# Sparse attention into a token mix: stores and loads of x by 32 rows, a second tile of normalised sums, another order of heads, and the mix's first steps in the attention's written order

## The chip, the cores and the metric

One core of one Trainium2 chip. The metric is device microseconds of one execution; lower is better. A core has TensorE (PE, with its weight loads PEld), VectorE (DVE), ScalarE (ACT), GpSimd (POOL) and SyncE (SP), which here only issues DMAs. All of them run their own queue in order and meet at semaphores.

## The reference

```python
scores = scale * np.matmul(q, k.transpose(0, 1, 3, 2))      # 4 batches, 8 heads, 768 x 64
mask = np.abs(blk_i - blk_j) <= 1                            # blocks of 32: 24 of them
mask |= (blk_i == 0) | (blk_j == 0) | (blk_i == 23) | (blk_j == 23)
# and three sampled key blocks for every query block
attn = softmax(where(mask, scores, -1e9));  x = attn @ v     # x: 4 x 768 x 512, heads side by side
theta = x @ w_theta;  zr, zi = x * cos(theta), x * sin(theta)
y = einsum('ts,bsd->btd', w_tok_r, zr) + einsum('ts,bsd->btd', w_tok_i, zi)
u = x + y;  out = u + np.maximum(u @ w_ch, 0.0)
```

## The kernel before

**Attention.** Two batches and eight heads are worked on together (bp = 0, 1). The eight heads are four positions p with two halves e each. A *unit* is one query block i of 32 rows (i = 1 to 22) over at most eight key blocks, or a *wide* unit: the first and last query block, which see all 768 keys, for one batch b and two positions. Per bp there are four wide units, then 22 units that go in pairs (odd i, then even i). The loop over n (from L449) is written out by hand under `manual_schedule()`, and each engine's queue has exactly this order. In an iteration: `load_q` (SP); `gather_k` of unit n+2 (POOL copies kg<-kb, L243); `scale_q` (DVE, L217); `scores` of unit n+1 (PE, S, L282, then the minimum m on DVE, L285); for odd i `values` of the pair before (PE, X, L333); `weights` of unit n+1 (ACT, exponentials P, L294); `turn` of unit n (PE transposes T, L300, and the ACT copy to pT, L302); a share of decoding the mix's weights (`Decoder`, pieces of 512 KB loaded at L59, then DVE and ACT); `finish` of the pair before; `load_pair` (va, SP, L262) and `gather_v` (vb, an indirect DMA of POOL, L265).

`finish` normalises X on DVE into the tile xo (L315 to L319, one buffer, `bufs=1`) and stores it to the DRAM tensor xs by two DMAs, one for each half c of the partitions (L350). Each has 64 rows of 2 KB, and its DRAM side has as its outermost dimension the two query blocks. `finish_wide` does the same for the wide units (L405), with the first and the last block outermost. X has one buffer as well, T one, S two, pT one, vb four, va two.

The layout of xs is `[bp, block, c, 32 rows, b, pp, 128]` with p = 2 pp + c. Keys come by `load_k` (L222) into kb, one buffer for the bp's 3 MB: the loads for bp = 1 stand at the top of the iteration in which the unit after next is the first wide one, behind the stores of the pair before, and wait for POOL's last copy out of the old keys.

**Mix.** `token_mix` is a generator. Its first part, up to the `yield`, loads x for steps 0 and 1 (`load_raw`: tile xr, four DMAs, L560; `load`: tile xa, four DMAs of 128 rows of 512 bytes with four blocks as outermost dimension, L547), transposes xr on DVE (`turn`, L576, then ACT and DVE for the high and low part), loads ACT's Sin table (L534) and does `theta` (PE, h, L586 to L588). A step is 128 tokens and 256 channels; there are 48. The attention calls this part at its end, after it has given back kb's and the scores' memory (L513, L514); there the written order no longer holds, and a planner places the instructions by its own estimates, also between those of the attention's last iterations. The rest of the mix (`mix`, PE, y, L624 to L626; `out`, L647 to L649) follows under the planner, in memory that the attention's other tiles leave.

`Tables` prepares the sampled block numbers at the start, in tiles of its own (DVE on sb_raw, L149 to L167).

Of the kernel before, what the change touches and what calls it, by code (L numbers as in the profile page):

```python
# [24 lines left out]
VB_BUFS = 4  # L25
Q_BUFS = 3
RAW_AHEAD = 6

# [88 lines left out]
class Tables:  # L117


    def __init__(self, nc, cp, sampled):  # L120
        self.raw = cp.tile([P, NB * 6], I32, name="sb_raw")
        nc.sync.dma_start(self.raw, sampled.rearrange("i k -> (i k)").partition_broadcast(P))

    def make(self, nc, cp):
        raw = self.raw
        words = raw.rearrange("p (i k w) -> p i k w", k=3, w=2)
        given = cp.tile([P, 3, NB], F32, name="sb_given")
        nc.vector.tensor_copy(given, words[:, :, :, 0].rearrange("p i k -> p k i"))
        r = cp.tile([P, 3, NB], F32, name="sb_r")
# [3 lines left out]
        iota_i = cp.tile([P, NB], I32, name="iota_i")  # L133
        nc.gpsimd.iota(iota_i, pattern=[[1, NB]], base=0, channel_multiplier=0)
        qi = cp.tile([P, NB], F32, name="qi")
# [6 lines left out]
        first_i = cp.tile([96, NP], I32, name="first_i")  # L142
        for k in range(3):
            nc.gpsimd.iota(first_i[32 * k : 32 * k + 32], pattern=[[768, NP]], base=0, channel_multiplier=1)
        first = cp.tile([96, NP], F32, name="first_row")
        nc.gpsimd.tensor_copy(first, first_i)

        u, t = raw.bitcast(F32).rearrange("p (x k i) -> x p k i", x=2, k=3)
        nc.vector.tensor_tensor(u, r, given, op=ALU.not_equal)  # L149
        nc.vector.tensor_tensor(t, r, qi.unsqueeze(1).to_broadcast([P, 3, NB]), op=ALU.subtract)  # L150
        nc.vector.tensor_tensor(t, t, t, op=ALU.mult)
        nc.vector.scalar_tensor_tensor(u, t, 1.5, u, op0=ALU.is_lt, op1=ALU.max)
        nc.vector.scalar_tensor_tensor(t, r, float(NB - 1), r, op0=ALU.subtract, op1=ALU.mult)
        nc.vector.scalar_tensor_tensor(u, t, 0.0, u, op0=ALU.is_equal, op1=ALU.max)
        for k in range(1, 3):
            for j in range(k):
                nc.vector.tensor_tensor(t[:, j, :], r[:, k, :], r[:, j, :], op=ALU.is_equal)
                nc.vector.tensor_tensor(u[:, k, :], u[:, k, :], t[:, j, :], op=ALU.max)

        for k in range(3):  # L160
            g = slice(32 * k, 32 * k + 32)
            nc.vector.tensor_scalar(t[g, 0, :], u[g, k, :], -1.0, 1.0, op0=ALU.mult, op1=ALU.add)
            for bp in range(NP):
                nc.vector.tensor_scalar(t[g, 1 + bp, :], r[g, k, :], 32.0, first[g, bp : bp + 1], op0=ALU.mult, op1=ALU.add)
        left, base = t[0:96, 0:1, :], t[0:96, 1:3, :]
        nc.vector.scalar_tensor_tensor(base, base, -ZEROS, left.to_broadcast([96, NP, NB]), op0=ALU.add, op1=ALU.mult)
        nc.vector.tensor_scalar(rows[0:96], base, ZEROS, None, op0=ALU.add)  # L167


def attention(tc, qT, qE, kT, vr, sampled, xs, ident, pieces, follow):  # L170
# [8 lines left out]
    nc = tc.nc  # L179
    with ExitStack() as ctx, ExitStack() as early:  # L180
# [3 lines left out]
        ps_s = early.enter_context(tc.tile_pool(name="ps_s", bufs=2, space=PSUM, side="right"))  # L184
        gp = ctx.enter_context(tc.tile_pool(name="gp", bufs=1))
# [33 lines left out]
        def load_k(bp, b, pp):  # L219
            if (b, pp) == (0, 0):  # L220
                kbs[bp] = kp.tile([P, 8, NB, 32], F32, tag="kb", name=f"kb{bp}")
            nc.sync.dma_start(kbs[bp][:, 4 * b + 2 * pp : 4 * b + 2 * pp + 2], kT[bp, b][:, 2 * pp : 2 * pp + 2])  # L222

        def load_edges(bp):
# [47 lines left out]
        def scores(bp, i):  # L272
# [5 lines left out]
            for b in range(2):  # L278
                for p in range(4):
                    for e in range(2):  # L280
                        rows = slice(64 * e, 64 * e + 64)
                        nc.tensor.matmul(sc[32 * p : 32 * p + 32, e, b, :], q[rows, b, p, :], keys[rows, :, :, 4 * b + p, :], start=True, stop=True)  # L282
            m = wp.tile([P, 2, 2], F32, tag="m", name=f"m{bp}_{i}", bufs=3)
# [28 lines left out]
        def normalised(name, x, n):  # L312
# [3 lines left out]
            nc.vector.reciprocal(sm, sm)  # L316
            xo = wp.tile([P, 8, 64], F32, tag="xo", name=f"xo{name}", bufs=1)[:, 0:n]
            by = sm.rearrange("r (b g) -> r b g", g=4).unsqueeze(3).to_broadcast([P, n // 4, 4, 64])
# [8 lines left out]
        def values(bp, i):  # L327
            x = st[bp, i]["X"] = sums_tile(f"{bp}_{i}")
            va = vas[((i - 1) // 2) % VA_BUFS]
            def weigh(b, e, p, c, u0, n, v, start, stop):  # L330
                r0 = 64 * (p % 2) + 32 * u0
                v0 = 65 * (8 * b + 4 * (p // 2) + 2 * e + p % 2)
                nc.tensor.matmul(  # L333
                    x[r0 : r0 + 32 * n, b, 2 * (p // 2) + e, :], pT_pair[:, 4 * c + 2 * e + b, p, u0 : u0 + n, :], v[:, v0 : v0 + 65],
                    start=start, stop=stop,
                )

            for e in range(2):
                for pp in range(2):
                    heads = [(b, e, 2 * pp + c) for b in range(2) for c in range(2)]  # L340
                    for head in heads:
# [5 lines left out]
        def finish(bp, i):  # L347
            xo = normalised(f"{bp}_{i}", st.pop((bp, i))["X"], 8)
            for c in range(2):
                nc.sync.dma_start(xs[bp, i : i + 2, c].rearrange("u q b p f -> u q (b p f)"), xo[64 * c : 64 * c + 64])  # L350

# [8 lines left out]
        def scores_wide(bp, b, pp):  # L360
            qe, kb = qes[bp], kbs[bp]
            scs = [ps_s.tile([P, 2, 2, 256], F32, tag="S", name=f"SW{bp}_{b}{pp}{e}").rearrange("r x y f -> r (x y f)") for e in range(2)]
            for c0, n in ((0, 16), (16, 8)):
                for c in range(2):
                    for e in range(2):
                        rows, p = slice(64 * e, 64 * e + 64), 2 * pp + c
                        nc.tensor.matmul(  # L367
                            scs[e][64 * c : 64 * c + 64, 32 * c0 : 32 * (c0 + n)], qe[rows, b, p, :], kb[rows, 4 * b + p, c0 : c0 + n, :],
                            start=True, stop=True,
# [29 lines left out]
        def finish_wide(bp, b, pp):  # L399
            if b == 0:  # L400
                load_v_wide(bp, 1, pp)
            if pp == 1:
                xo = normalised(f"{bp}_w{b}", xws[bp][:, b : b + 1], 4)
                for c in range(2):
                    nc.sync.dma_start(xs[bp, 0 : NB : NB - 1, c, :, b].rearrange("z q p f -> z q (p f)"), xo[64 * c : 64 * c + 64])  # L405

# [27 lines left out]
        with tc.manual_schedule():  # L434
            load_edges(0)
            load_k(0, 0, 0)
            tab = Tables(nc, cp, sampled)
            turn_edges(0)
# [9 lines left out]
            do(0, weights, weights_wide)  # L448
            for n in range(len(units) + 1):  # L449
                phases = 0  # L450
                if n < len(units):
# [40 lines left out]
                else:  # L492
# [9 lines left out]
                    else:  # L502
                        turn(bp, i)
                        do(n + 1, weights, weights_wide)
                    decoder.go(phases)
                    if last:
                        finish(*last)
# [4 lines left out]
            assert not decoder.left(), decoder.left()  # L512
        early.close()  # L513
        next(follow)  # L514


def token_mix(tc, w, ch_pieces, xs, outT, bias, nb):
# [8 lines left out]
    with ExitStack() as late, ExitStack() as ctx:  # L526
        xp = ctx.enter_context(tc.tile_pool(name="xp", bufs=3, side="right"))
        tz = ctx.enter_context(tc.tile_pool(name="tz", bufs=2, side="right"))
        tps = [ctx.enter_context(tc.tile_pool(name="tp0", bufs=1, side="right"))]
        ps_h = ctx.enter_context(tc.tile_pool(name="ps_h", bufs=3, space=PSUM, side="right"))  # L530
        ps_o = ctx.enter_context(tc.tile_pool(name="ps_o", bufs=1, space=PSUM, side="right"))

        half_pi, up_int, down_int, early = bias
        tc.keep_in_program_order(nc.scalar.activation(early, half_pi, AF.Sin))  # L534
        xa, xr, xT, angles, zs, us, ys = {}, {}, {}, {}, {}, {}, {}
# [5 lines left out]
        def load(k):  # L541

            b, h, j = at(k)
            xa[k] = xp.tile([P, 4, 4, 32], F32, tag="xa", name=f"xa{k}")
            for p in range(4):
                src = xs[b // 2, 4 * j : 4 * j + 4, p % 2, :, b % 2, p // 2]
                nc.sync.dma_start(xa[k][:, p].rearrange("s c u -> s (c u)"), src)  # L547

        def load_raw(k, pool=None):
# [8 lines left out]
            for p in range(4):  # L558
                src = xs[b // 2, 4 * j : 4 * j + 4, p % 2, :, b % 2, p // 2].rearrange("i q c -> q i c")
                nc.sync.dma_start(xr[b, j][32 * p : 32 * p + 32].rearrange("r i c u -> r i (c u)"), src)  # L560
# [95 lines left out]
        for k in range(2):  # L656
            load_raw(k, xp)
            load(k)
        turn(0)
        turn(1)  # L660
        theta(0)
        theta(1)
# [122 lines left out]
```

## Time and profile before

| what | value |
|---|---|
| median of the three runs shown | 686.46 us (680.64, 686.46, 686.54) |
| time of the profiled execution | 681.48 us |
| its span (first to last instruction) | 679.7 us |
| mean granted TensorE clock | 0.924 |
| busy: PE, PEld, DVE, ACT, POOL | 576.1, 501.7, 448.6, 334.9, 140.6 us |
| moved by DMA | 95.57 MB, mean 141 GB/s |

All rows below are of that one execution, in us from the span's start. In the groups a row reads: line, engine, operation, tile written <- tiles read, shapes, count | busy us, mean ns of one | idle us just before them, and what ended that idle time. The chain of waits is followed back from the last instruction: start, duration, what. A timeline row is start, duration, engine, line, operation, with the idle time before it in brackets. A stretch (A:B) gives its length, then busy us and count of each engine, the granted clock, the mean busy share of the DMA engines, and GB/s.

### The profile page before, as it was taken

The page shows a single profiled execution, that of the slowest core. Times are in us where ns is not written, and L with a number is a line of the kernel's source. Part 1 is how long each engine was busy: PE and PEld are TensorE (multiplying, and loading weights), DVE is VectorE, ACT ScalarE, POOL GpSimd, SP SyncE. Part 2 cuts the span into 40 slices and gives each one's busy share as a digit, 9 for nine tenths or more (in the row PEclk, how much of TensorE's full clock was granted, in tenths as well). Part 3 has the DMA queues.
Part 4 walks back from the last instruction along what each step waited for, and adds up shares of the span by engine and source line. Part 5 has one row for each costly group of instructions (what it writes and reads, how often), then busy time and mean ns, then how long its engine had stood idle before and what let it go on. Part 6 is the DMA issues. An engine that isn't in the chain of part 4 may idle for free.

```text
span 679.7 us, 16671 instructions
## 1 busy us (share of the span) xinstructions
PE 576.1 (85%) x6592; PEld 501.7 (74%) x6592; DVE 448.6 (66%) x1063; ACT 334.9 (49%) x708; POOL 140.6 (21%) x262
## 2 busy tenths in 40 slices
PE   4788767585878777774879999999999999999996
PEld 2466445462655545543769999999999999999996
DVE  3797775463777657655389979666586765846654
ACT  3466546362656455544266575345553455533520
POOL 1457546322247454620000000000000000000000
PEclk9989789786989879995769999999999999999999
DMA  8778668665579656742344323421133211121102
GB/s 300 257 224 237 212 208 261 219 213 191 175 231 274 194 180 201 250 140 78 92 123 120 107 56 83 123 78 59 48 95 108 68 58 47 60 69 62 31 0 94
DMA packets 71110, 95.57 MB, mean 141 GB/s; under 512 B 5240, under 2 KB 52984, under 8 KB 71032
## 3 DMA queue, kind: packets, MB, share of 16 engines
q1 hardware_dynamic: 64696, 71.08, 33.3%
q0 software_dynamic: 6336, 23.43, 10.6%
q8 instruction: 52, 0.85, 0.5%
q14 instruction: 26, 0.21, 0.1%
HBM read 81.90 MB, written 12.58 MB: 139 GB/s over the span
## 4 chain that ended last, share of the span: by engine, by line
PE 48%; DMA 34%; DVE 10%; SPq 3%; ACT 3%; issue 2%; DVEq 0%; ACTq 0%
DMA xs<-xo 26%; PE y L624 9%; PE y L625 9%; PE y L626 9%; PE h L588 3%; PE h L586 3%; PE h L587 3%; PE o L647 3%; PE o L648 3%; PE o L649 3%; PE SW L367 3%; DMA kb<-in_kT_dram 2%; DVE xo L319 2%; SPq L350 2%; DMA va<-in_vr_dram 1%
## 5 line engine op out<-in xcount | busy, mean ns | idle before, releaser
L243 POOL COPY kg<-kb 128x256 f32 (+2 forms) x202 | 94.9, 510 | 62.2 <-PE S L282 25.7
L294 ACT ACTIVATE P<-S,m 128x256 f32<-128x256 f32 x176 | 69.1, 477 | 77.4 <-DVE m L285 69.9
L300 PE MATMUL T<-ident,P 128*128 128x128 f32 x352 | 56.3, 312 | 19.9 <-ACT pT L302 19.4
L586 PE MATMUL h<-w_theta_hi,xTh 128*128 128x256 f32 x192 | 56.7, 295 | 14.9 <-ACT P L294 11.7
L624 PE MATMUL y<-w_tok_r_hi,zh 128*128 128x384 f32 x192 | 66.1, 344 | 3.7 <-DVE xo L319 3.3
L300 PEld LDWEIGHTS T<-ident,P 128*128 128x128 f32 x352 | 45.1, 160 | 31.9 <-ACT pT L302 28.9
L333 PE MATMUL X<-vb,pT 128*32 128x65 f32 x1408 | 45.0, 244 | 24.9 <-DVE xo L319 24.8
L625 PE MATMUL y<-w_tok_r_lo,zh 128*128 128x384 f32 x192 | 65.6, 342 | 0.0
L626 PE MATMUL y<-w_tok_r_hi,zl 128*128 128x384 f32 x192 | 64.8, 337 | 0.0
L625 PE MATMUL y<-w_tok_i_lo,zh 128*128 128x384 f32 x192 | 64.7, 337 | 0.0
L624 PE MATMUL y<-w_tok_i_hi,zh 128*128 128x384 f32 x192 | 64.7, 337 | 0.0
L265 POOL DMA_INDIRECT vb<-in_vr_dram,rows x44 | 43.8, 995 | 93.0 <-PE X L333 87.4
L626 PE MATMUL y<-w_tok_i_hi,zl 128*128 128x384 f32 x192 | 62.2, 334 | 0.0
L302 ACT COPY pT<-T 128x1024 f32<-128x1024 f32 x44 | 44.9, 1020 | 33.5 <-PE T L300 33.2
L285 DVE TENSOR_REDUCE m<-S 128x2 f32<-128x512 f32 x88 | 56.2, 680 | 5.9 <-PE S L282 5.9
L333 PEld LDWEIGHTS X<-vb,pT 128*32 128x32 f32 x1408 | 28.5, 119 | 42.0 <-DVE xo L319 32.0
L319 DVE TENSOR_TENSOR xo<-X,sm 128x512 f32<-128x512 f32 x22 | 15.2, 692 | 64.9 <-DMA xs<-xo 62.7
L588 PE MATMUL h<-w_theta_hi,xTl 128*128 128x256 f32 x192 | 56.3, 293 | 1.4 <-DVE xTl L578 1.4
L587 PE MATMUL h<-w_theta_lo,xTh 128*128 128x256 f32 x192 | 56.0, 292 | 0.0
L282 PE MATMUL S<-kg,q 64*32 64x256 f32 x1408 | 53.0, 410 | 3.3 <-DVE q L217 2.0
L586 PEld LDWEIGHTS h<-w_theta_hi,xTh 128*128 128x128 f32 x192 | 38.3, 199 | 16.1 <-ACT P L294 11.9
L333 PE MATMUL X<-va,pT 128*64 128x65 f32 x704 | 44.6, 255 | 0.7 <-DMA va<-in_vr_dram 0.6
(127 smaller groups left out, 1303.6 us busy)
## 6 DMA issues: line engine op xcount, KB each, us to landing
xa<-xs SPq DMA_DIRECT2D x192, 64.0 KB
vw<-in_vr_dram SPq DMA_DIRECT2D x8, 780.0 KB
kb<-in_kT_dram SPq DMA_DIRECT2D x8, 768.0 KB
xr<-xs SPq DMA_DIRECT2D x96, 64.0 KB
out_dram<-of SPq DMA_DIRECT2D x32, 192.0 KB
va<-in_vr_dram SPq DMA_DIRECT2D x22, 260.0 KB
q<-in_qT_dram SPq DMA_DIRECT2D x22, 256.0 KB
xs<-xo SPq DMA_DIRECT2D x44, 128.0 KB
```

Of the source, the lines that this page charges most:

```text
L243: nc.gpsimd.tensor_copy(dst, blocks.rearrange("r g s f -> r s g f"))
L282: nc.tensor.matmul(sc[32 * p : 32 * p + 32, e, b, :], q[rows, b, p, :], keys[rows, :, :, 4 * b + p, :], start=True, stop=True)
L285: nc.vector.tensor_reduce(m[:, e], sc[:, e], axis=AX.X, op=ALU.min)
L294: nc.scalar.activation(pt[:, e, b, :], sc[:, e, b, :], AF.Exp, bias=m[:, e, b : b + 1], scale=-1.0)
L300: nc.tensor.transpose(t[:, k, :], pt, ident)
L333: nc.tensor.matmul(x[r0 : r0 + 32 * n, b, 2 * (p // 2) + e, :], pT_pair[:, 4 * c + 2 * e + b, p, u0 : u0 + n, :], v[:, v0 : v0 + 65], star ...
L586: nc.tensor.matmul(ps, hi[:, c, :], wh[:, c, :], start=c == 0, stop=False)
L587: nc.tensor.matmul(ps, hi[:, c, :], wl[:, c, :], start=False, stop=False)
L588: nc.tensor.matmul(ps, lo[:, c, :], wh[:, c, :], start=False, stop=c == 3)
L624: nc.tensor.matmul(acc, zh[:, dd], wh[:, j, tt], start=j == 0 and m == 0, stop=False)
L625: nc.tensor.matmul(acc, zh[:, dd], wl[:, j, tt], start=False, stop=False)
L626: nc.tensor.matmul(acc, zl[:, dd], wh[:, j, tt], start=False, stop=j == 5 and m == 1)
```

## The change

- `xo` gets two buffers. To make room, the tables' short-lived tiles become parts of one `scratch` tile that takes one of them at the start.
- Each store of `finish` and `finish_wide` is cut into two of 32 rows: four DMAs a pair in place of two, each with the 32 rows as outermost dimension on the DRAM side.
- Heads are numbered p = 2 c + pp in place of 2 pp + c, so that in xs the two pp of a row stand side by side; keys and values are laid out on the host to match, and `place(b, p)` finds a head's keys.
- `load` goes by blocks: four DMAs of 32 rows with two runs of 1 KB, in place of four with 128 rows of 512 bytes.
- kb's memory is given back at the top of the last iteration but one, and the mix's first loads (steps 0 and 1) are written there. The scores' PSUM is given back after the last unit's decoding, and `turn` and `theta` of steps 0 and 1, with the Sin table's load between, are written there, ahead of the last pair's `values` and `finish`.

```diff
-        self.raw = cp.tile([P, NB * 6], I32, name="sb_raw")
+        self.scratch = wp.tile([P, 8, 64], F32, tag="xo", name="sb_scratch", bufs=XO_BUFS).rearrange("p g d -> p (g d)")
+        self.raw = self.part(0, NB * 6).bitcast(I32)
...
+        def place(b, p):
+
+            return 4 * b + 2 * (p % 2) + p // 2
...
-            xo = wp.tile([P, 8, 64], F32, tag="xo", name=f"xo{name}", bufs=1)[:, 0:n]
+            xo = wp.tile([P, 8, 64], F32, tag="xo", name=f"xo{name}", bufs=XO_BUFS)[:, 0:n]
...
             for c in range(2):
-                nc.sync.dma_start(xs[bp, i : i + 2, c].rearrange("u q b p f -> u q (b p f)"), xo[64 * c : 64 * c + 64])
+                for u in range(2):
+                    r0 = 64 * c + 32 * u
+                    nc.sync.dma_start(xs[bp, i + u, c].rearrange("q b p f -> q (b p f)"), xo[r0 : r0 + 32])
...
             for n in range(len(units) + 1):
+                if n == len(units) - 2:
+                    early.close()
+                    next(follow)
...
                     decoder.go(phases)
+                    if n == len(units) - 1:
+                        scored.close()
+                        next(follow)
                     if last:
                         finish(*last)
...
-        early.close()
-        next(follow)
...
-            for p in range(4):
-                src = xs[b // 2, 4 * j : 4 * j + 4, p % 2, :, b % 2, p // 2]
-                nc.sync.dma_start(xa[k][:, p].rearrange("s c u -> s (c u)"), src)
+            for i in range(4):
+                src = xs[b // 2, 4 * j + i, :, :, b % 2].rearrange("c q p f -> q c (p f)")
+                dst = xa[k][32 * i : 32 * i + 32].rearrange("s (c p) x u -> s c (p x u)", c=2)
+                nc.sync.dma_start(dst, src)
...
         for k in range(2):
             load_raw(k, xp)
             load(k)
+        yield
+        ps_h = ctx.enter_context(tc.tile_pool(name="ps_h", bufs=3, space=PSUM, side="right"))
+        ps_o = ctx.enter_context(tc.tile_pool(name="ps_o", bufs=1, space=PSUM, side="right"))
         turn(0)
         turn(1)
+        nc.scalar.activation(early, half_pi, AF.Sin)
         theta(0)
         theta(1)
         yield
```

More of the change, by code (lines that the diff above doesn't have):

```diff
@@ L26 @@
 Q_BUFS = 3
+XO_BUFS = 2
 RAW_AHEAD = 6
@@ L117, with __init__, part @@
 class Tables:
-    def __init__(self, nc, cp, sampled):
-        self.raw = cp.tile([P, NB * 6], I32, name="sb_raw")
+    def __init__(self, nc, wp, sampled):
+        self.scratch = wp.tile([P, 8, 64], F32, tag="xo", name="sb_scratch", bufs=XO_BUFS).rearrange("p g d -> p (g d)")
+        self.raw = self.part(0, NB * 6).bitcast(I32)
         nc.sync.dma_start(self.raw, sampled.rearrange("i k -> (i k)").partition_broadcast(P))
+    def part(self, c0, n):
+        return self.scratch[:, c0 : c0 + n]
     def make(self, nc, cp):
@@ L126, in make @@
         words = raw.rearrange("p (i k w) -> p i k w", k=3, w=2)
-        given = cp.tile([P, 3, NB], F32, name="sb_given")
+        given = self.part(144, 72).rearrange("p (k i) -> p k i", k=3)
         nc.vector.tensor_copy(given, words[:, :, :, 0].rearrange("p i k -> p k i"))
-        r = cp.tile([P, 3, NB], F32, name="sb_r")
+        r = self.part(216, 72).rearrange("p (k i) -> p k i", k=3)
         nc.vector.tensor_scalar(r, given, 0.0, float(NB - 1), op0=ALU.max, op1=ALU.min)
@@ L132, in make @@
         nc.vector.tensor_copy(self.block.rearrange("p (i k) -> p k i", k=3), r[0:1])
-        iota_i = cp.tile([P, NB], I32, name="iota_i")
+        iota_i = self.part(288, NB).bitcast(I32)
         nc.gpsimd.iota(iota_i, pattern=[[1, NB]], base=0, channel_multiplier=0)
-        qi = cp.tile([P, NB], F32, name="qi")
+        qi = self.part(312, NB)
         nc.gpsimd.tensor_copy(qi, iota_i)
@@ L141, in make @@
             nc.gpsimd.memset(rows[96:128, :, i], int(ZEROS))
-        first_i = cp.tile([96, NP], I32, name="first_i")
+        first_i = self.part(336, NP)[0:96].bitcast(I32)
         for k in range(3):
             nc.gpsimd.iota(first_i[32 * k : 32 * k + 32], pattern=[[768, NP]], base=0, channel_multiplier=1)
-        first = cp.tile([96, NP], F32, name="first_row")
+        first = self.part(338, NP)[0:96]
         nc.gpsimd.tensor_copy(first, first_i)
@@ L179, in attention @@
     nc = tc.nc
-    with ExitStack() as ctx, ExitStack() as early:
+    with ExitStack() as ctx, ExitStack() as scored, ExitStack() as early:
         ep = early.enter_context(tc.tile_pool(name="ep", bufs=1, side="right"))
         kp = early.enter_context(tc.tile_pool(name="kp", bufs=1, side="right"))
-        ps_s = early.enter_context(tc.tile_pool(name="ps_s", bufs=2, space=PSUM, side="right"))
+        ps_s = scored.enter_context(tc.tile_pool(name="ps_s", bufs=2, space=PSUM, side="right"))
         gp = ctx.enter_context(tc.tile_pool(name="gp", bufs=1))
@@ L281, in scores @@
                         rows = slice(64 * e, 64 * e + 64)
-                        nc.tensor.matmul(sc[32 * p : 32 * p + 32, e, b, :], q[rows, b, p, :], keys[rows, :, :, 4 * b + p, :], start=True, stop=True)
+                        nc.tensor.matmul(sc[32 * p : 32 * p + 32, e, b, :], q[rows, b, p, :], keys[rows, :, :, place(b, p), :], start=True, stop=True)
             m = wp.tile([P, 2, 2], F32, tag="m", name=f"m{bp}_{i}", bufs=3)
@@ L329, in values, with weigh @@
             va = vas[((i - 1) // 2) % VA_BUFS]
-            def weigh(b, e, p, c, u0, n, v, start, stop):
-                r0 = 64 * (p % 2) + 32 * u0
-                v0 = 65 * (8 * b + 4 * (p // 2) + 2 * e + p % 2)
+            def weigh(b, e, p, k, u0, n, v, start, stop):
+                c, pp = p // 2, p % 2
+                r0 = 64 * c + 32 * u0
+                v0 = 65 * (8 * b + 4 * pp + 2 * e + c)
                 nc.tensor.matmul(
-                    x[r0 : r0 + 32 * n, b, 2 * (p // 2) + e, :], pT_pair[:, 4 * c + 2 * e + b, p, u0 : u0 + n, :], v[:, v0 : v0 + 65],
+                    x[r0 : r0 + 32 * n, b, 2 * pp + e, :], pT_pair[:, 4 * k + 2 * e + b, p, u0 : u0 + n, :], v[:, v0 : v0 + 65],
                     start=start, stop=stop,
@@ L339, in values @@
                 for pp in range(2):
-                    heads = [(b, e, 2 * pp + c) for b in range(2) for c in range(2)]
+                    heads = [(b, e, 2 * c + pp) for b in range(2) for c in range(2)]
                     for head in heads:
@@ L365, in scores_wide @@
                     for e in range(2):
-                        rows, p = slice(64 * e, 64 * e + 64), 2 * pp + c
+                        rows, p = slice(64 * e, 64 * e + 64), 2 * c + pp
                         nc.tensor.matmul(
-                            scs[e][64 * c : 64 * c + 64, 32 * c0 : 32 * (c0 + n)], qe[rows, b, p, :], kb[rows, 4 * b + p, c0 : c0 + n, :],
+                            scs[e][64 * c : 64 * c + 64, 32 * c0 : 32 * (c0 + n)], qe[rows, b, p, :], kb[rows, place(b, p), c0 : c0 + n, :],
                             start=True, stop=True,
@@ L404, in finish_wide @@
                 for c in range(2):
-                    nc.sync.dma_start(xs[bp, 0 : NB : NB - 1, c, :, b].rearrange("z q p f -> z q (p f)"), xo[64 * c : 64 * c + 64])
+                    for z in range(2):
+                        r0 = 64 * c + 32 * z
+                        nc.sync.dma_start(xs[bp, (NB - 1) * z, c, :, b].rearrange("q p f -> q (p f)"), xo[r0 : r0 + 32])
         WIDE = [(b, pp) for b in range(2) for pp in range(2)]
@@ L436, in attention @@
             load_k(0, 0, 0)
-            tab = Tables(nc, cp, sampled)
+            tab = Tables(nc, wp, sampled)
             turn_edges(0)
@@ L558, in load_raw @@
             for p in range(4):
-                src = xs[b // 2, 4 * j : 4 * j + 4, p % 2, :, b % 2, p // 2].rearrange("i q c -> q i c")
+                src = xs[b // 2, 4 * j : 4 * j + 4, p // 2, :, b % 2, p % 2].rearrange("i q c -> q i c")
                 nc.sync.dma_start(xr[b, j][32 * p : 32 * p + 32].rearrange("r i c u -> r i (c u)"), src)
@@ L758 @@
     va[..., :64] = np.asarray(v).reshape(NP, 2, 2, 4, 768, 64).transpose(0, 4, 1, 2, 3, 5)
-    va = va.reshape(NP, 768, 2, 2, 2, 2, 65).transpose(0, 1, 2, 4, 3, 5, 6)
+    va = va.reshape(NP, 768, 2, 2, 2, 2, 65).transpose(0, 1, 2, 5, 3, 4, 6)
     turned = np.arange(512).reshape(2, 4, 2, 32).transpose(0, 2, 1, 3).reshape(-1)
@@ L764 @@
         "qE": np.ascontiguousarray(qh[:, :, :, [0, NB - 1]].transpose(0, 1, 2, 4, 5, 3, 6)).reshape(NP, P, 512),
-        "kT": np.ascontiguousarray(rows_by_head(k).transpose(0, 4, 1, 2, 5, 3, 6)).reshape(NP, 2, P, 4, NB, 32),
+        "kT": np.ascontiguousarray(rows_by_head(k).transpose(0, 4, 1, 2, 5, 3, 6)[:, :, :, :, [0, 2, 1, 3]]).reshape(NP, 2, P, 4, NB, 32),
         "vr": np.concatenate([va.reshape(NP * 768, 1040), np.zeros((32, 1040), np.float32)]),
```

3 lines of the change are left out of this document (removed).

## The prediction

> **What bounds it now.** I read the page first. Its chain that ended last gives a quarter of the span to one transfer, the store of the attention's result, and the groups put nearly the same time ahead of the instruction that fills the tile it reads.
>
> ```profile
> span 679.7 us, 16671 instructions
> ...
> GB/s 300 257 224 237 212 208 261 219 213 191 175 231 274 194 180 201 250 140 78 92 123 120 107 56 83 123 78 59 48 95 108 68 58 47 60 69 62 31 0 94
> ...
> PE 48%; DMA 34%; DVE 10%; SPq 3%; ACT 3%; issue 2%; DVEq 0%; ACTq 0%
> DMA xs<-xo 26%; PE y L624 9%; PE y L625 9%; PE y L626 9%; PE h L588 3%; PE h L586 3%; PE h L587 3%; PE o L647 3%; PE o L648 3%; PE o L649 3%; PE SW L367 3%; DMA kb<-in_kT_dram 2%; DVE xo L319 2%; SPq L350 2%; DMA va<-in_vr_dram 1%
> ...
> L319 DVE TENSOR_TENSOR xo<-X,sm 128x512 f32<-128x512 f32 x22 | 15.2, 692 | 64.9 <-DMA xs<-xo 62.7
> ...
> out_dram<-of SPq DMA_DIRECT2D x32, 192.0 KB
> va<-in_vr_dram SPq DMA_DIRECT2D x22, 260.0 KB
> ...
> xs<-xo SPq DMA_DIRECT2D x44, 128.0 KB
> ```
>
> Then the chain in order of time, here one pair of query blocks:
>
> ```profile
> 96.89 0.70 DVE xo L319
> 97.61 0.51 SPq L350
> 98.18 8.10 DMA xs<-xo
> 106.40 0.70 DVE xo L319
> ```
>
> There is one xo tile. VectorE fills it (0.70), SP issues the store (0.51), the store lands 8.10 us later, and only then may VectorE fill it for the next pair. The loop of a pair is this ring and nothing else, though two DMAs of 128 KB are a small load. Cut into stages, the trace says how full the engines are meanwhile:
>
> ```profile
> core 0: us, PE busy (x) PEld busy (x) DVE busy (x) ACT busy (x) POOL busy (x), PEclk, DMA share, GB/s
> 51.21:145.28 94.07, 71.55 (x1464) 50.12 (x1456) 58.78 (x108) 49.63 (x96) 50.95 (x93) 0.84 0.70 222
> ...
> 209.09:298.91 89.82, 68.59 (x1448) 47.52 (x1448) 57.20 (x107) 48.84 (x95) 51.52 (x91) 0.91 0.66 210
> 298.91:327.44 28.53, 13.61 (x232) 11.47 (x232) 15.07 (x39) 12.82 (x27) 0.00 (x0) 0.75 0.31 88
> 327.44:357.00 29.56, 24.16 (x107) 22.78 (x108) 18.43 (x61) 12.09 (x29) 0.00 (x0) 0.67 0.40 112
> 357.00:676.00 319.00, 317.17 (x1983) 316.21 (x1981) 220.36 (x594) 152.79 (x365) 0.00 (x0) 1.00 0.24 71
> ```
>
> The first two rows begin and end at an xo and hold nine pairs each: 183.89 us for 18, so 10.22 us a pair, with TensorE busy 76% at a granted clock under 1. The next two rows are the hand-over to the mix: 58 us in which TensorE is part idle and part slow. From 357 on TensorE is full at clock 1.00; nothing in this change touches that work.
>
> **The change, part by part.**
>
> *Two tiles and stores by 32 rows.* The wait ahead of xo goes if a store lands within two periods less filling and issue. How fast the new stores land the trace doesn't show; the bounds are a store of 192 KB at the quiet end of the kernel and a load of 260 KB inside the pair stage:
>
> ```profile
> 300.78 9.42 DMA va<-in_vr_dram
> ...
> 672.54 1.85 DMA out_dram<-of
> ```
>
> Both are far under 2 x 8.5 - 1.2 = 15.8 us, so I cost the store at nothing; the cover is the second tile, and without it a landing of 1.85 to 9.42 would still set a ring of 3.1 to 10.6 us. The two further issues of a pair are 2 x 0.51 = 1.0 us on SP; the va, q and weight loads queued behind are prefetched by one pair or more.
>
> What is late next? After X, TensorE transposes, ScalarE copies to pT, and this a second time; the next X needs the second copy. First a pair that came out of the wide stage without a wait for xo, from X to X (columns as above), then one whose X began after a wait:
>
> ```profile
> 203.58:211.01 7.43, 7.30 (x184) 5.16 (x177) 6.92 (x15) 5.99 (x13) 4.54 (x8) 1.00 0.91 266
> ```
>
> ```profile
> 256.42 0.38 PE L333 MATMUL X<-vb,pT 128*32 128x65 f32 x7 [1.08 <-DVE xo L319]
> ...
> 264.25 1.02 ACT L302 COPY pT<-T 128x1024 f32<-128x1024 f32 x1 [0.72 <-PE T L300]
> ```
>
> The first went from X to X in 7.43 us with TensorE busy 7.30: the floor. In the second the copy ends at 265.27, 8.85 us after X began, and with the hop to TensorE the ring is 8.95; part of that is an exponential made late by the old wait. Between 7.43 and 8.95 I take **8.5**, nearer the upper row, because VectorE works in order and is already busy 6.92 of 7.43. So 18 x (10.22 - 8.5) = **-31** (bounds -50 and -23).
>
> By the Trainium skill (DMA: Bandwidth & Descriptors, "Why a DMA increments its semaphore by 16 and not by 1") a transfer is split over the largest number of engines up to 16 that divides the slowest dimension of both sides. By that rule the old store, whose slowest dimension is the 2 blocks, runs on two engines, the new one with 32 rows on sixteen; 128 KB landing in 8.10 us against 192 KB in 1.85 agrees. The same page ("Rules for kernel authors") advises against cutting transfers in halves and calls those under 64 KB mostly overhead; by that rule the four stores of a pair gain nothing over two, which two tiles would still hide, and the sum would stand.
>
> *Hand-over inside the attention.* The keys of the second half wait on SP behind the held-up store:
>
> ```profile
> 141.70 1.42 POOL L243 COPY kg<-kb 128x256 f32<-128x256 f32 x4
> ...
> 146.00 1.05 SPq L350 DMA_DIRECT2D xs<-xo  x2
> ...
> 147.78 3.17 SPq L222 DMA_DIRECT2D kb<-in_kT_dram  x4
> ...
> 159.44 2.96 PE L367 MATMUL SW<-kb,qe 64*64 64x512 f32 x16 [8.95 <-DMA kb<-in_kT_dram]
> ```
>
> POOL has read the old keys at 143.12; the load leaves 4.66 us later, because the store ahead of it waited for xo. Now it can leave at once, and it finds a shorter queue than the 128 KB twice that left 1.7 us before it. Of the 8.95 us that TensorE stood, I take **-8** (-4.7 if only the issue moves, -9 at most).
>
> *The mix's first steps in the fixed order.* The planner had put them where VectorE meets the load before it has landed:
>
> ```profile
> 301.49 3.10 SPq L560 DMA_DIRECT2D xr<-xs  x4
> ...
> 311.18 0.89 DVE L576 STREAM_TRANSPOSE r<-xr 128x128 f32<-128x128 f32 x4 [8.26 <-DMA xr<-xs]
> ```
>
> VectorE stands 8.26 us for xr; behind it wait a minimum, the exponentials, and TensorE, in the view of who waited for whom (us in total, times, longest):
>
> ```profile
> PE h L586 <- ACT P L294: 11.7, 1, 11.7
> ```
>  After the change the 16 loads leave at the top of the last iteration but one and the transposes come at the end of the last, about a pair later. What they cost SP (ns, shortest, median, longest), and the landing of xr:
>
> ```profile
> L547 SPq DMA_DIRECT2D xa<-xs x192: 507/508/1477, 304.6 to 635.7; - x192
> L560 SPq DMA_DIRECT2D xr<-xs x96: 302/430/1612, 301.5 to 524.7; - x96
> ```
>
> ```profile
> 312.24 3.21 DMA xr<-xs
> ```
>
> Eight of each are 8 x 0.51 + 8 x 0.43 = 7.5 us of SP ahead of the stores of that pair, for which only the fill after next waits; kb has been read by then. The landing is bounded by 3.21 us and the 9.42 above.
> With 7.5 of issue and 3.21 that is 10.7 us after the top, so a stall of 1 to 3 us may be left ahead of theta. I take **-10** of 11.7 (bounds -6 and -12). The Sin table's load keeps its place behind the last exponential.
>
> *The start of the mix.* SP stands at the first weight load of the mix for the last store, whose memory it takes over:
>
> ```profile
> 328.74 7.69 DMA xs<-xo
> 336.45 0.35 SPq L59
> ```
>
> A store that lands in 1.85 to 9.42 us gives 6 back or takes 2; in 327.44 to 357 that delay is on the chain up to xr and theta. The xa loads change from 512-byte to 1 KB runs with as many issues. I take **-6** (0 to -13, the latter if TensorE's clock of 0.67 there also recovers).
>
> *At nothing:* the order of heads (same matmul shapes, same bytes), and the tables in a borrowed xo tile. Their VectorE work is on the chain at 18 to 21 us; waits that sharing one tile may add are bounded by a second pass over it, below 3 us:
>
> ```profile
> 18.24 0.76 DVE sb_raw L164 x2
> 19.01 0.55 DVE sb_raw L162
> 19.56 0.69 DVE sb_raw L164 x2
> 20.59 0.49 DVE sb_raw L164 x2
> ```
>
> **Sum.** -31 - 8 - 10 - 6 = -55. The profiled execution took 681.48 us (679.7 of span and 1.8 around it): 626.5. The three runs shown are 680.64, 686.46 and 686.54, so the median lies 5 above it; I allow 1.5 for that and say **628**.
>
> **Rivals.**
>
> *A, VectorE and POOL bind at once.* Without the pauses of the ring the engines collide more. For it: VectorE is busy 58.78 us in nine pairs, 6.5 a pair, and 7.43 was a single pair. At 9.4 us a pair the stage gives -15, the rest -6, -8 and -3: 32 off, **649**.
>
> *B, everything runs at its floor.* 7.43 a pair gives -50, then -9, -12 and -10: 81 off, **600**. For it: the pair at 203.58; against: only one such.
>
> *C, the stores still set the pace.* If what takes 8 us is not the shape of the store but the queue it stands in, two tiles only put two stores in line and the pair stays at 10.22. For it: the va load of 260 KB needs 9.42 us in the same stage. Against: va has 1% of the chain, so its landings are seldom late. Then only -5, -10 and 0 remain: **666**.
>
> *D, slower: the loads lose their rate.* The stores, now among all loads, could take the memory's time from the gathers. A pair moves 94.07 us x 222 GB/s / 9 = 2.32 MB. The other terms give 24 us, 1.3 a pair, so this decides from 11.6 us a pair on, which is 200 GB/s. At 175, the lowest slice of the attention ahead of its hand-over to the mix in the page's row, it would be 13.3 us: +55 - 24 = +31, **712**. Against it: 266 GB/s in the stretch at 203.58, with stores in it.
>
> **How the numbers follow.** Forecast 0.60, A 0.18, B 0.12, C 0.07, D 0.03. A measurement of this kernel tells about 1% from no change. D alone ends above that bound; C is the nearest to no change, and a part of it could come out within 1%. Faster 0.95, same 0.02, slower 0.03. The forecast's own terms with their bounds reach from 597 (all best) to 650; with A inside and B's edge the range is 604 to 656.
>
> **What would show it.** Right: no wait of xo for the store, xo to xo about 8.5 us with clock near 1, kb issued as soon as POOL's last copy ends and no stand of TensorE ahead of SW, no stand of VectorE for xr, the mix full some 55 us earlier, at about 302. Wrong: waits of X for pT or of VectorE for q that add up to the old 62.7 us; pair rows at 10 us with the store's landing as long as before (C); or a new stand of theta for xr of over 5 us.

## The result, and the profile after

The changed kernel takes 616.78 us (median of 613.46, 616.68, 616.88 and 619.75), beside 686.5 us for the kernel before on the same chip: a ratio of 0.901 (95% interval 0.893 to 0.909). It is faster by 70 us; the forecast was 58. The profiled execution is the one of 619.75 us.

The page of the changed kernel (span, chain by engine and by line, two groups, issues with KB and us to landing):

```profile
span 617.6 us, 16759 instructions
...
GB/s 293 271 211 263 275 286 317 244 319 128 238 237 288 269 277 287 203 103 158 142 117 44 70 136 99 57 52 47 92 132 73 48 52 47 77 64 54 18 0 103
...
PE 66%; DVE 13%; DMA 10%; ACT 6%; SPq 3%; issue 2%; DVEq 0%; ACTq 0%
PE y L639 10%; PE y L641 10%; PE y L640 10%; PE X L343 4%; DVE m L294 4%; PE S L291 3%; PE h L603 3%; PE h L601 3%; DMA q<-in_qT_dram 3%; PE SW L379 3%; PE h L602 3%; PE o L662 3%; PE o L664 3%; PE o L663 3%; PE T L309 3%; ACT pT L311 2%
...
xa<-xs SPq DMA_DIRECT2D x192, 64.0 KB, 1.9
vw<-in_vr_dram SPq DMA_DIRECT2D x8, 780.0 KB, 10.0
...
va<-in_vr_dram SPq DMA_DIRECT2D x22, 260.0 KB, 6.0
q<-in_qT_dram SPq DMA_DIRECT2D x22, 256.0 KB, 6.5
xs<-xo SPq DMA_DIRECT2D x88, 64.0 KB, 5.2
```

The chain is TensorE's for 66% of the span (48% before), and the DMAs have 10% in place of 34%. The store, which had 26% alone, is not among its lines any more: twice as many of them land in 5.2 us each, less than a pair takes. The view of the line that fills xo has nothing left under the idle time ahead of it, where 62.7 us for the store had stood:

```profile
L328 DVE TENSOR_TENSOR xo<-X,sm x22: 691/692/692, 51.5 to 274.4; 128x512 f32<-128x512 f32 x22
...
its engine sat idle before it (us, times) until:
who waited for it (us, times):
...
```

By stages, cut at the same fills of xo as before (first to ninth, ninth to twelfth, twelfth to twentieth, twentieth to last, last to end), and from 295 on:

```profile
core 0: us, PE busy (x) PEld busy (x) DVE busy (x) ACT busy (x) POOL busy (x), PEclk, DMA share, GB/s
51.47:124.18 72.71, 63.41 (x1445) 44.17 (x1443) 61.25 (x109) 47.41 (x95) 56.52 (x93) 0.95 0.90 280
124.18:185.94 61.76, 47.48 (x833) 32.41 (x834) 43.90 (x79) 34.94 (x59) 20.26 (x35) 0.92 0.72 229
185.94:251.40 65.46, 59.29 (x1408) 41.45 (x1408) 60.67 (x106) 45.23 (x92) 53.70 (x89) 1.00 0.92 277
251.40:274.42 23.02, 16.58 (x272) 13.29 (x272) 16.22 (x39) 15.26 (x30) 1.55 (x3) 0.85 0.48 141
274.42:617.60 343.18, 334.81 (x2088) 333.70 (x2088) 239.41 (x653) 165.70 (x397) 0.00 (x0) 1.00 0.25 77
...
295.00:614.00 319.00, 316.62 (x1980) 316.10 (x1978) 223.01 (x600) 155.13 (x372) 0.00 (x0) 1.00 0.24 71
```

Against the rows of before:

| stage | before | after | difference |
|---|---|---|---|
| up to the first xo | 51.21 | 51.47 | +0.3 |
| pairs, first half | 94.07 | 72.71 | -21.4 |
| hand-over to the second half, wide units | 63.81 | 61.76 | -2.0 |
| pairs, second half | 89.82 | 65.46 | -24.4 |
| last two pairs, start of the mix | 28.53 | 23.02 | -5.5 |
| last xo to the end | 352.26 | 343.18 | -9.1 |
| span | 679.7 | 617.6 | -62.1 |

The two rows of pairs hold 45.7 of the 62.1 us. In them the DMA engines are now 0.90 and 0.92 busy (0.70 and 0.66 before) at 280 and 277 GB/s, VectorE 84% and 93%, TensorE 87% and 91% at a clock of 0.95 and 1.00. The mix is full from 295 on, where it was from 357.

What is late now stands in the chain in order of time and in the timeline (the idle time before an instruction in brackets):

```profile
98.87 10.00 DMA vw<-in_vr_dram
...
108.89 11.86 DMA q<-in_qT_dram
```

```profile
117.04 0.70 PE L343 MATMUL X<-va,pT 128*64 128x65 f32 x8 [3.98 <-DMA va<-in_vr_dram]
...
120.77 0.43 DVE L222 TENSOR_SCALAR q<-q 128x512 f32<-128x512 f32 x1 [7.69 <-DMA q<-in_qT_dram]
...
122.03 2.40 POOL L252 COPY kg<-kb 128x256 f32<-128x256 f32 x4
...
124.90 2.05 SPq L362 DMA_DIRECT2D xs<-xo  x4
127.05 0.47 SPq L271 DMA_DIRECT2D va<-in_vr_dram  x1
127.62 2.40 SPq L227 DMA_DIRECT2D kb<-in_kT_dram  x4
...
136.28 2.96 PE L379 MATMUL SW<-kb,qe 64*64 64x512 f32 x16 [4.92 <-DMA kb<-in_kT_dram]
```

The two vw loads of 780 KB for the wide units meet the last pairs' q and va; one q lands after 11.86 us, where the median is 6.5, and VectorE stands for it. By the view of what SP's issues waited for, SP itself stood until a vw had landed, once before a store and once before this q (us in total, times, longest); why it had to, nothing here shows:

```profile
SPq L362 <- DMA vw<-in_vr_dram: 4.1, 1, 4.1
...
SPq L216 <- DMA vw<-in_vr_dram: 1.8, 1, 1.8
```

And TensorE still stands for the new keys, 4.92 us where it was 8.95.

### The profile page after: what moved, and what is told of

Read it like the earlier page. It is cut to its first block, busy times and chain, and to the rows that moved or that the text cites. A ratio compares the mean times of both kernels' runs of the same rounds, so it can differ in the third digit from the quotient of the medians.

```text
span 617.6 us, 16759 instructions
## 1 busy us (share of the span) xinstructions
PE 558.7 (90%) x6592; PEld 488.9 (79%) x6592; DVE 455.7 (74%) x1063; ACT 333.7 (54%) x708; POOL 150.3 (24%) x262
## 4 chain that ended last, share of the span: by engine, by line
PE 66%; DVE 13%; DMA 10%; ACT 6%; SPq 3%; issue 2%; DVEq 0%; ACTq 0%
PE y L639 10%; PE y L641 10%; PE y L640 10%; PE X L343 4%; DVE m L294 4%; PE S L291 3%; PE h L603 3%; PE h L601 3%; DMA q<-in_qT_dram 3%; PE SW L379 3%; PE h L602 3%; PE o L662 3%; PE o L664 3%; PE o L663 3%; PE T L309 3%; ACT pT L311 2%
## 5 line engine op out<-in xcount | busy, mean ns | idle before, releaser
L252 POOL COPY kg<-kb 128x256 f32 (+2 forms) x202 | 104.5, 557 | 57.9 <-PE S L291 25.8
L309 PE MATMUL T<-ident,P 128*128 128x128 f32 x352 | 49.9, 286 | 16.8 <-ACT pT L311 16.1
L309 PEld LDWEIGHTS T<-ident,P 128*128 128x128 f32 x352 | 39.3, 145 | 28.9 <-ACT pT L311 26.6
L601 PE MATMUL h<-w_theta_hi,xTh 128*128 128x256 f32 x192 | 55.4, 289 | 2.5 <-ACT xTh L592 2.4
L605 ACT ACTIVATE t<-h,up_int 128x256 f32<-128x256 f32 x48 | 22.7, 473 | 53.7 <-PE h L603 51.8
L291 PE MATMUL S<-kg,q 64*32 64x256 f32 x1408 | 50.2, 392 | 0.0
L343 PE MATMUL X<-vb,pT 128*32 128x65 f32 x1408 | 43.6, 231 | 1.7 <-issue 1.7
L343 PE MATMUL X<-va,pT 128*64 128x65 f32 x704 | 40.8, 239 | 4.0 <-DMA va<-in_vr_dram 4.0
L663 PE MATMUL o<-ul,w_ch_hi 128*128 128x384 f32 x128 | 42.8, 334 | 0.0
L664 PE MATMUL o<-uh,w_ch_lo 128*128 128x384 f32 x128 | 42.8, 334 | 0.0
```

Of the source, the lines that this page charges most:

```text
L252: nc.gpsimd.tensor_copy(dst, blocks.rearrange("r g s f -> r s g f"))
L309: nc.tensor.transpose(t[:, k, :], pt, ident)
L343: nc.tensor.matmul(x[r0 : r0 + 32 * n, b, 2 * pp + e, :], pT_pair[:, 4 * k + 2 * e + b, p, u0 : u0 + n, :], v[:, v0 : v0 + 65], start=star ...
L601: nc.tensor.matmul(ps, hi[:, c, :], wh[:, c, :], start=c == 0, stop=False)
```

## The experiments

The kernel before was timed beside each on the same chip, at a median of 686.2 to 687.7 us. T1 takes the shape of the store, which the prediction mentioned, though its sum went by the second tile: a store whose outermost dimension is 2 is slow itself and sets the pace. T2 is its rival: what counted was that one tile made every pair wait for its store. Pair means one sixteenth of the two pair stages; a dash stands where no stage was compared.

| kernel | median us | ratio to before, 95% | pair | last xo to end |
|---|---|---|---|---|
| after | 616.78 | 0.893 to 0.909 | 8.64 | 343.2 |
| one tile | 620.69 | 0.901 to 0.908 | 8.55 | 344.4 |
| stores by 64 rows, two tiles | 672.56 | 0.976 to 0.987 | 10.88 | 352.4 |
| stores by 64 rows, one tile | 683.63 | 0.995 to 1.003 | 11.58 | 352.9 |
| mix's first steps at the end | 621.72 | 0.902 to 0.913 | 8.55 | 346.9 |
| before, stores by 32 rows only | 630.72 | 0.914 to 0.931 | 8.49 | 351.8 |
| outermost 2 | 663.57 | 0.958 to 0.975 | 10.75 | 344.6 |
| outermost 4 | 627.14 | 0.907 to 0.923 | 9.02 | 341.3 |
| xa loads as before | 623.31 | 0.901 to 0.916 | 8.72 | 348.9 |
| vw loads early | 612.94 | 0.888 to 0.898 | 8.27 | 343.9 |
| q scaled on ScalarE | 614.61 | 0.884 to 0.898 | - | - |
| both | 612.20 | 0.885 to 0.897 | 8.37 | 344.2 |
| less decoding | 605.23 | 0.876 to 0.890 | 8.38 | 341.6 |

**Tiles against shape.** One tile, the old stores, and both:

```diff
-XO_BUFS = 2
+XO_BUFS = 1
```

```diff
-                for u in range(2):
-                    r0 = 64 * c + 32 * u
-                    nc.sync.dma_start(xs[bp, i + u, c].rearrange("q b p f -> q (b p f)"), xo[r0 : r0 + 32])
+                nc.sync.dma_start(xs[bp, i : i + 2, c].rearrange("u q b p f -> u q (b p f)"), xo[64 * c : 64 * c + 64])
...
```

> The changed kernel with one xo tile again; the stores stay cut by 32 rows. Theory 1 (the old store is slow because of its shape, its outermost dimension of 2 blocks keeping it on few of the DMA engines): the stores still land in about 5 us, so the ring of one tile is fill 0.7 + four issues 2.0 + landing 5.2 = about 8 us, under the 8.64 us that a pair takes after the change; uneven pairs cost about 0.5 us each, 16 x 0.5 = 8: about 625 us, 616 to 636. Theory 2 (the landing is the queue the store stands in, and the second tile is what helps): the ring of 10 to 12 us is back and the time is 655 to 670.

> The changed kernel with the old stores of 64 rows (two blocks outermost), two xo tiles kept. Theory 1: the few engines that carry the stores become the pace, a pair takes 10 to 11 us, 16 x (10.5 - 8.64) = 30 us more: 640 to 660 us, with landings of 8 us and more. Theory 2: two tiles hide the landing, 612 to 622 us.

> The changed kernel with the old stores and one tile: what is left of the change is the order of heads, the loads of x and the fixed order. Both theories: the old ring of a pair is back (16 x (11.49 - 8.64) = 46 us more than the changed kernel), so about 662 us, 655 to 672; the distance to the kernel before, 15 to 25 us, is what the fixed order and the loads bring.

With quick stores one tile costs 4 us, which the overlapping intervals don't tell from nothing; with the old stores the second tile brings 11 (672.56 against 683.63, intervals apart). The cut is worth 56 us with two tiles and 63 with one. So T2 falls. T1 has the direction, but it too had the old stores with two tiles at 660 at most, and with one tile at 672 at most. The waits of that kernel with two tiles (us in total, times, longest), and the row of q in the same view of the changed kernel, with its longest wait behind, show why:

```profile
DVE q L222 <- DMA q<-in_qT_dram: 44.2, 13, 9.5
...
PE X L343 <- DMA va<-in_vr_dram: 24.8, 9, 7.0
```

```profile
DVE q L222 <- DMA q<-in_qT_dram: 9.9, 3, 7.7
```

xo doesn't wait for its store there, yet q and va come late by nearly as much: the slow store also delays the loads that run beside it. They land late, and are not just issued late: the chain of that kernel with two tiles has 12.31 us for a q and 13.28 for a va from issue to landing, where the medians after the change are 6.5 and 6.0.

```profile
56.74 12.31 DMA q<-in_qT_dram
...
84.82 13.28 DMA va<-in_vr_dram
```

With one tile the wait is at xo again, and the rest of the change, which that kernel has whole, brings nothing that can be measured (0.995 to 1.003):

```profile
DVE xo L328 <- DMA xs<-xo: 74.3, 18, 8.7
```

**The cut alone**, the kernel before with four stores a pair:

> The kernel before with nothing changed but its stores: cut by 32 rows. One tile, old order of heads, old loads, the planner's hand-over. Theory 1 (the shape of the store is the whole cause): within 1.5% of the changed kernel with one tile, which took 620.7: 618 to 632. Rival: the order of heads and the loads of x by 32 rows carry a part that shows only once the stores are quick: 633 to 650.

It gives 55 of the 70 us (630.72 against 686.17), and its pair takes 8.49 us. The other edits, without the second tile, are worth some 10 us together (against the changed kernel with one tile, 620.69, intervals apart), and in the profiles the difference lies behind the last xo: 351.8 against 344.4.

**How many rows stand outermost.** Stores of 32 rows as in the changed kernel, whose rows are walked with 2 or 4 as the outermost dimension (the rows of a block reach xs in another order, so the output is no longer the reference's; the work stays the same):

```diff
-                    nc.sync.dma_start(xs[bp, i + u, c].rearrange("q b p f -> q (b p f)"), xo[r0 : r0 + 32])
+                    nc.sync.dma_start(xs[bp, i + u, c].rearrange("(h l) b p f -> l h (b p f)", l=OUTER), xo[r0 : r0 + 32])
...
```

> The changed kernel (two tiles, four stores of 32 rows of 2 KB a pair); only the order in which a store walks the rows differs, so that its DRAM side has an outermost dimension of 2 with 16 rows each. The rows of a block land in another order, so the output is not the reference's; bytes, runs and number of DMAs are the same. Theory 1 (the outermost dimension sets the number of DMA engines, here 2): as slow as with the stores of 64 rows and two tiles, 672.6: 660 to 680. Rival (what counts is that a store has 32 rows, or one block): 613 to 622.

> The same with an outermost dimension of 4 with 8 rows each (the rows of a block land in another order, so the output is not the reference's). Theory 1: the stores run on 4 engines, half the load on each of that with 2. The 10 to 11 us of a pair at 2 engines are made of the stores' share and the loads' share; with half the stores' share about 7.5 to 8, so the pair's other work binds again: 615 to 632. Rival: the same time as with 2.

Same count of stores, same bytes, same tiles: 663.57, 627.14 and 616.78 us for 2, 4 and 32. What the store's engines do can be counted on the page as packets, first of the kernel with 2, then with 4, then the changed one:

```profile
DMA packets 61230, 95.58 MB, mean 144 GB/s; under 512 B 7648, under 2 KB 43104, under 8 KB 61152
```

```profile
DMA packets 61438, 95.58 MB, mean 153 GB/s; under 512 B 7856, under 2 KB 43312, under 8 KB 61360
```

```profile
DMA packets 62686, 95.59 MB, mean 155 GB/s; under 512 B 9104, under 2 KB 44560, under 8 KB 62608
```

There are 88 + 16 = 104 such stores, those of the wide units included. From 2 to 4 the packets under 512 B grow by 208, which is 2 a store; from 4 to 32 by 1248, which is 12 a store. So with 7440 of other DMAs a store has 2, 4 and 16 of them. The count also fits the kernel before, with 52 stores, and the one with the cut alone: from 5240 to 6800 they grow by 104 x 16 - 52 x 2 = 1560.

```profile
DMA packets 71110, 95.57 MB, mean 141 GB/s; under 512 B 5240, under 2 KB 52984, under 8 KB 71032
```

```profile
DMA packets 72671, 95.59 MB, mean 153 GB/s; under 512 B 6800, under 2 KB 54544, under 8 KB 72592
```

The trace doesn't name these packets; read as one for each engine that takes part, they give 2, 4 and 16 engines. By the Trainium skill (DMA: Bandwidth & Descriptors, "Why a DMA increments its semaphore by 16 and not by 1") that is the number of engines that such shapes give, and the runs agree. The Trainium skill's advice against two transfers for two halves (same page, "Rules for kernel authors") gives as its reason that both halves run on all sixteen engines. That isn't so for the store before, by the counts above, and here the cut alone took 55 us off. With two engines, q and va wait as in the 64-row kernel (the view of the waits of that with 2):

```profile
DVE q L223 <- DMA q<-in_qT_dram: 43.1, 12, 8.9
...
PEld X L344 <- DMA va<-in_vr_dram: 28.8, 8, 6.7
```

This kernel and the one with stores of 64 rows and two tiles both run their stores on two engines, and their pairs are alike (10.75 and 10.88 us), but 9 us lie between them (663.57 and 672.56, intervals apart). In the profiles these stand behind the last xo (344.6 and 352.4); what the size of a store does there isn't shown.

**The mix's first steps and xa.** The first kernel gives kb's memory back after the loop and leaves the placing to the planner; the second loads xa by four DMAs of 128 rows of 512 bytes:

```diff
-                if n == len(units) - 2:
-                    early.close()
-                    next(follow)
...
-                    if n == len(units) - 1:
-                        scored.close()
-                        next(follow)
...
+        early.close()
+        scored.close()
+        next(follow)
...
```

```diff
...
+            for p in range(4):
+                src = xs[b // 2, 4 * j : 4 * j + 4, p // 2, :, b % 2, p % 2]
+                nc.sync.dma_start(xa[k][:, p].rearrange("s c u -> s (c u)"), src)
```

> The changed kernel with the mix's first loads and products handed to the planner at the end of the attention again. If the fixed order is worth what the hand-over shows (5.5 us less from the last but one xo to the last, and the old stand of VectorE for xr of 8.3 us and of TensorE of 11.7 us comes back): 6 to 12 us more, 622 to 630 us. Rival: with stores that land quickly and x loads on all engines the planner's order no longer meets a late xr, and the time is within 3 us of the changed kernel.

> The changed kernel with the loads of xa as before: four DMAs of 128 rows of 512 bytes, outermost dimension of 4 blocks (heads stay in their new order). If the loads at the start of the mix are held back by few engines: 3 to 8 us more, 620 to 625, all of it between the last xo and the full mix. Rival: the mix has its loads early enough either way, within 3 us of the changed kernel.

Both overlap with the changed kernel. In their traces the planner's order costs 0.9 us in the stage of the last two pairs and 3.7 behind the last xo; its median, 4.9 us longer, falls between the two expectations. The old xa loads cost 5.7 us, behind the last xo. Each is about 1% or less, so the profiles locate them and the times don't prove them.

**What bounds the pair now.** q scaled on ScalarE; vw 16 and 10 iterations ahead in place of 8 (the edges 18); both; and last, as a probe, the decoding of the weights' low words left out, 48 us of VectorE's busy time of 456 (the low parts then lack what the decoding puts right):

```diff
-            nc.vector.tensor_scalar(t, t, -0.125, None, op0=ALU.mult)
+            nc.scalar.activation(t, t, AF.Copy, scale=-0.125)
```

```diff
-                if first_of_pair(n + 8):
+                if first_of_pair(n + 18):
                     load_edges(1)
-                    for pp in range(2):
+                for pp in range(2):
+                    if first_of_pair(n + 16 - 6 * pp):
                         load_v_wide(1, 0, pp)
```

> The changed kernel with the scaling of q moved from VectorE to ScalarE (one instruction of about 0.5 us a pair and its wait for the load). If VectorE, busy 93% of the pairs, is what binds now: 0.3 to 0.5 us a pair less, 22 pairs, 607 to 612. Rival: the pair is bound by the loads (the DMA engines' share is 0.90 to 0.92 there) or by TensorE's chain: within 3 us of 616.8, or slower where ScalarE stands for q.

> The changed kernel with the two loads of 780 KB for the wide units of the second half issued earlier and apart from each other (16 and 10 iterations ahead in place of both 8 ahead), the edge queries 18 ahead. If the pause of 7.7 us of VectorE for q at 113 to 121 us comes from these loads standing in one queue ahead of q: 4 to 7 us less, 610 to 613. Rival: the DMA engines are full there whatever the order, and the pause only moves: within 2 us.

> Both together: q scaled on ScalarE and the wide loads early and apart. If both theories hold, 601 to 607; if the loads alone bind, as the second alone; if neither, 614 to 618.

> The changed kernel without the decoding of the weights' low words: three VectorE instructions of a piece fall away (about 0.44 + 0.72 + 0.75 = 1.9 us a piece of the attention, 22 pieces, so 42 us of VectorE's work, some 1.5 us a pair, and half as much a piece for the 8 of the mix); all loads stay. The low part of the weights is left out of the products' second term, so the output is slightly off. If VectorE, 93% busy in the second pair stage, sets the 8.64 us of a pair: 1 us a pair and more, 595 to 602. If the DMA engines (share 0.90 to 0.92) set it: within 4 us of 616.8. With TensorE's floor of 7.4 a pair in the way: 600 to 606.

With early vw loads the 7.7 us pause is gone, and the first half's pairs take 65.5 us in place of 72.7. That the loads did this isn't shown: with the same loads and q on ScalarE the stage takes 70.6. The total, 612.94, isn't apart from 616.78, nor are the other two; both edits together missed their 601 to 607. Of the kernels that leave nothing out these three have the lowest medians. With less decoding the profiled executions stand 20 us apart (the medians 11.6, intervals apart): 5.4 of that up to the first xo (46.1 in place of 51.5), 10.9 in the wide stage (50.9 in place of 61.8), and only 4.1 in the pair stages. The first of these, by engines:

```profile
46.11:116.02 69.91, 62.98 (x1445) 43.60 (x1443) 49.21 (x90) 46.40 (x92) 49.18 (x94) 0.98 0.99 301
```

VectorE is 70% busy there and the pair hardly shorter; the DMA engines are at 0.99. So VectorE, which looked nearly full, doesn't set the pair alone. That the transfers take its place when it is relieved is likely from their share, but not tested, and what limits them, memory or engines, no run here separates.

## Why the prediction was right or wrong

**The ring of xo** was read rightly, and so was its end: no wait of xo is left, and the clock is at 0.95 and 1.00. The pair was forecast at 8.5 us and measured at 8.64.

**The term of the pairs, -31,** was mis-sized by a wrong count: "the first two rows begin and end at an xo and hold nine pairs each". They hold nine fills of xo, the ends included, so eight pairs. A pair took 183.89 / 16 = 11.49 us before, not 10.22, and 16 x (11.49 - 8.64) = -45.7. With the right count the forecast's own 8.5 would have given 16 x 2.99 = -48, and the sum 681.5 - 72 = 609.5. The same slip stands in rival D's 2.32 MB a pair (2.61).

**The two tiles as the cover** was the weaker part of the reasoning. A landing of 1.85 to 9.42 was bounded well (5.2 measured, 4.4 with one tile), and with the new stores one tile keeps the pair at 8.55 us, with some waits for the store left (the view of its xo line, us and times):

```profile
  DMA xs<-xo: 11.8, 6
```

So the sum credited the wrong part of the change: two tiles with the old stores end xo's wait too, but not the slow pair. The shape does the work, and it does it twice: it ends the ring, and it frees the loads. The second effect was not in the sum, and wasn't needed for the ring; but a kernel with two tiles and old stores, which the ring alone would have made quick, shows it (10.88 a pair).

**The hand-over inside the attention, -8,** gave -2.0. The step that failed is "now it can leave at once, and it finds a shorter queue". POOL has read the old keys at 124.43, and the load leaves at 127.62, 3.19 us later (4.66 before): the pair's stores and the va load stand ahead of it on SP, and VectorE, 7.69 us late through q, made them late. And the queue is fuller: the stretch from there on is at 0.94.

```profile
124.18:140.00 15.82, 10.05 (x165) 6.86 (x166) 7.70 (x15) 7.51 (x14) 1.21 (x2) 0.89 0.94 318
```

The size depends on the execution: three other kernels with the same code up to there (one tile aside) took 62.9, 58.8 and 56.0 us for the stage, with TensorE waiting 2.96, 1.55 and 0 us for kb. The term is -1 to -8, and -8 was its best case.

**The fixed order, -10,** is -5.5 in the stage of the last pairs. The timeline shows what was forecast: the loads leave at the top, r hardly waits, and theta is done before the last X.

```profile
255.67 2.43 SPq L575 DMA_DIRECT2D xr<-xs  x4
...
261.82 0.88 DVE L591 STREAM_TRANSPOSE r<-xr 128x128 f32<-128x128 f32 x4
264.86 0.89 DVE L591 STREAM_TRANSPOSE r<-xr 128x128 f32<-128x128 f32 x4 [0.72 <-DMA xr<-xs]
...
263.46 0.58 PE L601 MATMUL h<-w_theta_hi,xTh 128*128 128x256 f32 x1 [2.39 <-ACT xTh L592]
...
269.57 0.43 PE L343 MATMUL X<-vb,pT 128*32 128x65 f32 x16
```

TensorE's stand ahead of theta went from 11.65 to 2.39 us, within the forecast's "1 to 3 us may be left". Its idle time in the stage fell from 28.53 - 13.61 = 14.92 to 23.02 - 16.58 = 6.44, by 8.5; the stage shows 5.5, because 40 matmuls (3 us) that had run ahead of the held-up xo now run after it (272 matmuls in place of 232, and 1408 in place of 1448 in the pairs ahead of it). But the written order is not what did most of it. The two kernels that differ in this alone or nearly so, first the one with the cut alone under the planner, then the changed one without the written order, in the timeline:

```profile
261.87 0.58 PE L590 MATMUL h<-w_theta_hi,xTh 128*128 128x256 f32 x1 [6.84 <-ACT P L294]
```

```profile
257.75 0.58 PE L598 MATMUL h<-w_theta_hi,xTh 128*128 128x256 f32 x1 [6.20 <-ACT P L303]
```

So quick stores take the stand from 11.65 to 6.84 or 6.20, the order from there to 2.39; and of those last 4 us the stage keeps 0.9 (23.9 against 23.0). The prediction laid the whole stand to the place that the planner had chosen, and some of it was the store's.

**The start of the mix, -6,** is -9.1. With the old xa loads 5.7 of it are lost again. The last store on the chain, to which the prediction laid the term, took 7.69 us and takes 1.73:

```profile
278.24 1.73 DMA xs<-xo
```

By itself that store is worth little here: with stores of 32 rows on two engines the stage takes 344.6 us, 1.4 more than after the change. What came back as well is TensorE's clock, which the prediction kept for its bound: its row from 327.44 to 357 has 0.67, the first 20 us now have 0.92, and with the old xa loads a stretch of 10 us is at 0.66 again (first the changed kernel, then that one):

```profile
274.42:295.00 20.58, 18.19 (x110) 17.61 (x111) 15.80 (x53) 10.57 (x27) 0.00 (x0) 0.92 0.55 158
```

```profile
292.68:302.68 10.00, 8.00 (x35) 8.00 (x36) 8.67 (x29) 7.42 (x20) 0.00 (x0) 0.66 0.39 111
```

How much of the 9.1 us each part of the change brought isn't shown.

**The rivals.** A: the engines do collide (VectorE is busy 7.6 us a pair; by the right count it was 7.25 before, not 6.5), but at 8.64 and not 9.4. B's 7.43 was reached as a mean nowhere; the best stage of all these kernels has 63.4 / 8 = 7.9 (both edits). C, that it is the queue and not the shape, is refuted by outermost 2 and 4. D: the rate rose, from 222 to 280 GB/s. That the sum came so close is partly luck, since its errors cancel: 626.5 was forecast for the profiled execution and 619.75 came, which is -14.7 from the pairs, +6.0 and +4.5 from the two hand-overs, -3.1 from the start of the mix, +0.3 at the start and as much outside the span. The median lies 3 us below that execution, where the forecast had allowed 1.5 above; with these 4.5 the forecast of 628 is 11 too high.

**Open:** whether the fixed order, the second tile, early vw loads or q on ScalarE are worth anything, each being about 1% or less; what each part brought at the start of the mix; and what limits the transfers at a share of 0.9 to 0.99.

## What to carry to other kernels

Count how many rows stand outermost on the DRAM side of each small DMA, stores too: two there made 128 KB take 8 us and cost 8% of the kernel, and the profile page's count of packets under 512 B, compared between two kernels, tells how the number of engines changed. When a wait for a buffer goes away with a second buffer, ask whether the transfer behind it also holds others; here two tiles alone gained 11 us and moved the rest of the wait to q and va. And when a stage is cut from event to event, count the periods between, not the events.

## What the runs showed of the hardware that was not expected

A slow store delays loads that have nothing to do with it: with stores on two engines q's waits add up to 44.2 us and va's to 24.8, with stores on sixteen to 9.9 and 4.0, and loads that took 6.5 and 6.0 us then land after 12.31 and 13.28. Four engines are nearly enough for these stores: 627.14 us against 616.78, where two cost 663.57.
